# A planner's order table with one entry per task, token tiles laid one after another for layer A's transpose, and layer B's product as one operation per chunk

## The chip, the cores and the metric

The kernel runs on one core of one Trainium2 chip. Times are device microseconds (us) of one execution. The time before is a median of 360.13 us over 4 runs (359.67 to 361.37). One further reading of the same program is the profiled execution: the hardware profiler's trace of one run.

## The reference

The input x is 2048 tokens by 640 channels, in bf16. Four residual layers follow each other, A, B, A, B, each on a layer norm of x without learned factors. Both A layers have the same weights, and so have both B layers.

```python
x = x + A(layernorm(x)); x = x + B(layernorm(x))
x = x + A(layernorm(x)); x = x + B(layernorm(x))
# A: diagonal complex recurrence over the tokens
h_t = Lam_bar * h_{t-1} + B_bar @ u_t          # 640 complex states
A(u)_t = 2 * Re(C @ h_t) + Dskip * u_t
# B: gating by a signal that does not depend on x
kv = short_conv(B_k) * B_v                     # 4 taps per channel
y  = causal_conv(kv, ssm_k) + kv * ssm_D       # 2048 taps, by FFT in the reference
B(q) = q * y
```

So y is computed once and used by both B layers.

## The kernel before, in words

**Front part.** Tables of sines and cosines are made. k and v are loaded transposed, kv is formed by the short convolution (matmuls with diagonal matrices, L1064) and stored to memory. A's weights are transposed and combined on TensorE (L486, L501, L502, L522). The long convolution y is a two-stage transform over five groups of 128 channels, `yq0` to `yq4`: stage A (`KA`, `VA`, L1109, 64 columns a matmul), stage B (`KB`, `VB`, L1133 to L1138), the product of the spectra on VectorE (`pw`, L1190 to L1195), the inverse stages (`IB`, L1214 and L1215; a DMA transpose `tt`; `IA`, L1243), and a store (`st`). Every result of TensorE is copied out of one of four PSUM buffers by ScalarE (L296) or VectorE (L298).

**Layers.** x is cut into four chunks of 512 tokens, c0 to c3, each held as four tiles q = 0 to 3 of 128 tokens by 640 channels. `A1` and `A2` are the two A layers, `B1` and `B2` the two B layers. For one chunk, an A layer (`ALayer.chunk`) runs these tasks:

- `ln`: statistics. In A1 by batch-norm instructions on VectorE (`bn`, L620 and L621), elsewhere by squares summed on ScalarE (`nm`, `sq`, `sd`, L590 to L600); `post` on VectorE gives 1/std and -mean/std;
- `id`: the normalised tile, on ScalarE (L640) or VectorE (L642), written to a buffer `u`;
- `tu`: one DMA transpose of `u` to `uT` (L670), issued by SyncE;
- `bp`: three groups of matmuls with B_bar (L684, L687), 100 matmuls of 256 columns for a chunk; `ev` copies them out on ScalarE (L296);
- `ri`, `sc`, `cy`, `ro` on VectorE: a rotation (L706 to L708), two scans along the tokens (L722), the carry to the next chunk (L733 to L735), a rotation back (L745 to L747);
- `cp`: the output product for each tile (L773), 30 matmuls for an even tile and 25 for an odd one, two more in A1, where x is added on TensorE too;
- `xe`: the new x tile out of PSUM, with its sum (L781, L783, L785).

A B layer (`b_chunk`) runs `ln`, then `u` for each tile (the same normalisation, L640 or L642), then `m`: a product with y (L818, 128x640) and an addition of x (L820 with its sum in B1, L822 in B2). In the last chunk of B2 each tile is a group by itself, with two fused operations, L805 and L809. SyncE then stores the output (L828).

**What sets the order.** All of this is written down as tasks with dependencies, an engine (for copies, `id`, `u` and A1's `xe` a choice of two: ScalarE first, VectorE second) and an estimated duration. `Sched.run` (L179) is a list planner that runs while the kernel is built: it walks through planned time, and at each moment gives every free engine the ready task of the highest rank. A task with a choice goes to its second engine only if the first one is busy for 0.3 more planned us. The planner also gives out the shared buffers (13 of b5, 6 of b10, 4 PSUM). Then all tasks are emitted in the order of their planned starts. On the chip each engine executes its own list strictly in that order; an instruction whose inputs are late holds up everything behind it on that engine. The rank comes from the table `WHEN` (L52), which before has one number for each group: tasks whose names differ only behind a colon, such as the tiles of `A1c0_cp`, share one.

Of the kernel before, what the change touches and what calls it, by code (L numbers as in the profile page):

```python
# [9 lines left out]
ALU = mybir.AluOpType  # L10
# [23 lines left out]
TOK = 2 * NB  # L34
# [18 lines left out]
    "yt_io0": -1077.9, "yt_ph0": -1019.3, "yt_sin0": 190.5, "yt_neg0": 314.5, "yt_io6": -1435.7, "yt_ph6": -1019.8, "yt_sin6": -1080.4, "yt_neg6": 172.3,  # L53
    "yt_io12": 294.3, "yt_ph12": -1069.6, "yt_sin12": 375.6, "yt_neg12": 156.6, "yt_Ci": 118.7, "yt_Si": 403.1, "yt_nsi": 236.7, "yt_f0": -965, "yt_f2":
    -1540, "yt_f3": -1887, "yt_f4": 179, "yt_h0": 174.5, "yt_h1": 154.3, "yt_h2": 148.5, "yt_h3": 189.9, "kv_dsl": 34.9, "kv_kd": 410.2, "kv_k0": -1067.5,
    "kv_k1": 205.4, "kv_k2": 230.3, "kv_d0": -1030.9, "kv_d1": -1037.8, "kv_d2": 125.1, "kv_ds0": 95.3, "kv_lk0": -919.4, "kv_lv0": 119.4, "kv_mm0":
    -1408, "kv_ev0": 192.8, "kv_st0": -966.5, "kv_ds1": 400.8, "kv_lk1": 143.9, "kv_lv1": 406.3, "kv_mm1": 238.5, "kv_ev1": 232.1, "kv_st1": 180.1,
    "kv_ds2": -1696.5, "kv_lk2": 390.3, "kv_lv2": 173.4, "kv_mm2": 244.3, "kv_ev2": 403.7, "kv_st2": -1020, "kv_ds3": -1063.8, "kv_lk3": -1121.4,
    "kv_lv3": 669.8, "kv_mm3": 420.7, "kv_ev3": -1025, "kv_st3": 1400.2, "kv_ds4": 90.8, "kv_lk4": -926.2, "kv_lv4": 7.3, "kv_mm4": 33, "kv_ev4": -831.9,
    "kv_st4": -980.1, "a_pl": 481.2, "a_p0": -840.7, "a_p1": -1244.2, "a_p2": 1659, "a_p3": 156.5, "a_p4": -793.6, "a_p5": 225.8, "a_p6": -1643.5,  # L60
    "a_lamd": 156.7, "a_f": 165.3, "a_dd": 521.1, "a_ldB0": 150.8, "a_ldB1": -1247.6, "a_wl00": -1403.1, "a_wc00": -1264.8, "a_wm00": 209.8, "a_wl01":
    75.8, "a_wc01": -881, "a_wm01": 418.7, "a_wl02": 307.9, "a_wc02": 301.4, "a_wm02": 403.5, "a_wl03": 164, "a_wc03": -903.2, "a_wm03": -1083.3,
    "a_wl04": 357.2, "a_wc04": -1099.8, "a_wm04": 601.7, "a_b00": 178, "a_b0e0": 230.3, "a_b01": 173.9, "a_b0e1": -1067.1, "a_b10": 69.2, "a_b1e0":
    -1516.7, "a_b11": -1560.6, "a_b1e1": 508.8, "a_gm0": -1359.9, "a_ge0": -1048.3, "a_gm1": -727, "a_ge1": -1525.1, "a_gm2": -1618.5, "a_ge2": -1376.9,
    "a_gm3": -1641.8, "a_ge3": -1386.3, "a_gm4": -1643.2, "a_ge4": -1403, "a_wl10": -2.6, "a_wc10": 155, "a_wm10": -1068.5, "a_wl11": 159.1, "a_wc11":
    -965.4, "a_wm11": 184, "a_wl12": -818.1, "a_wc12": -1242.6, "a_wm12": 79.5, "a_wl13": 104.8, "a_wc13": 414.8, "a_wm13": 181.4, "a_wl14": -1008.6,
    "a_wc14": 26.2, "a_wm14": -1248.1, "a_ti": -1521.4, "a_ta": 395.3, "a_t0": -829.9, "a_t1": 170.8, "a_t2": 613.8, "yq0_kl": -982.4, "yq0_ka": -1602.5,
    "yq0_KA": 159.8, "yq0_KB": 402.8, "yq0_vl": -1113.3, "yq0_VA": 481.3, "yq0_VB": -1118.9, "yq1_kl": 30, "yq1_ka": 311.3, "yq1_KA": -1517.3, "yq1_KB":
    -954.5, "yq0_pw": 209.4, "yq0_IB": 298.2, "yq0_tt": -1552, "yq1_vl": 1519.1, "yq1_VA": -1096.8, "yq1_VB": 420.6, "yq0_IA": 407.6, "yq0_st": -1537.5,
    "yq2_kl": 435.6, "yq2_ka": 157.2, "yq2_KA": 277.9, "yq2_KB": -1166.2, "yq1_pw": 360.8, "yq1_IB": -871.2, "yq1_tt": -1130.5, "yq2_vl": -1467.1,  # L70
    "yq2_VA": 23.2, "yq2_VB": 25.8, "yq1_IA": -1377.8, "yq1_st": -1484.6, "yq3_kl": 498, "yq3_ka": 1686.9, "yq3_KA": 438.7, "yq3_KB": -1402.5, "yq2_pw":
    1355.7, "yq2_IB": -1302.1, "yq2_tt": -1424, "yq3_vl": -834.2, "yq3_VA": 161.1, "yq3_VB": 86.9, "yq2_IA": 2.9, "yq2_st": 300.2, "yq4_kl": -1275,
    "yq4_ka": 618.1, "yq4_KA": -931.8, "yq4_KB": 225.6, "yq3_pw": -1643.5, "yq3_IB": 331.5, "yq3_tt": -814.8, "yq4_vl": -798.8, "yq4_VA": 157.4, "yq4_VB":
    326.4, "yq3_IA": 628.2, "yq3_st": 404.5, "yq4_pw": 594.6, "yq4_IB": 599.4, "yq4_tt": -1071.8, "yq4_IA": 126.1, "yq4_st": -1404, "xl0": -1622.2,
    "A1c0_ln_bn": 302.5, "A1c0_ln_sd": -1096.7, "A1c0_ln_post": -1648.8, "A1c0_id": -1304.5, "A1c0_tu": -1475.7, "A1c0_bp": 10.7, "A1c0_ev": 355.4,
    "A1c0_ri": 62.1, "A1c0_sc": 641.6, "A1c0_cy": 233.1, "A1c0_ro": -1576.9, "A1c0_xr": 396.2, "A1c0_cp": 627.9, "A1c0_xe": -1443.8, "xl1": -978,
    "A1c1_ln_bn": 221, "A1c1_ln_sd": 479.8, "A1c1_ln_post": -942.2, "A1c1_id": 1422.5, "A1c1_tu": -1312.3, "A1c1_bp": 338.4, "A1c1_ev": 192.1, "A1c1_ri":
    1654.8, "A1c1_sc": -1000.3, "A1c1_cy": -1122.1, "A1c1_ro": -1077.3, "A1c1_xr": 627.3, "A1c1_cp": -1539.8, "A1c1_xe": -1077.9, "xl2": -1346.1,
    "A1c2_ln_bn": 611.3, "A1c2_ln_sd": -1123.4, "A1c2_ln_post": 402.2, "A1c2_id": 141, "A1c2_tu": 96.1, "A1c2_bp": 640.8, "A1c2_ev": -867.9, "A1c2_ri":
    22, "A1c2_sc": 40.1, "A1c2_cy": -1431.1, "A1c2_ro": -1012.6, "A1c2_xr": 471.5, "A1c2_cp": -1082.5, "A1c2_xe": -1450.9, "xl3": 672.8, "A1c3_ln_bn":  # L80
    37.8, "A1c3_ln_sd": -1392.7, "A1c3_ln_post": -1339.6, "A1c3_id": 30.4, "A1c3_tu": 252.1, "A1c3_bp": -1329.6, "A1c3_ev": 410.6, "A1c3_ri": -1152.5,
    "A1c3_sc": 383.7, "A1c3_ro": 185.7, "A1c3_xr": 534.8, "A1c3_cp": 257.2, "A1c3_xe": -1166.6, "yl0": 143.2, "B1c0_ln_nm": 627.2, "B1c0_ln_sq": 628.8,
    "B1c0_ln_sd": 604.7, "B1c0_ln_post": 185.1, "B1c0_u": -1662.7, "B1c0_m": 369.5, "A2c0_ln_nm": 202.2, "A2c0_ln_sq": 222, "A2c0_ln_sd": 59.4,
    "A2c0_ln_post": -1459.4, "A2c0_id": 273.5, "A2c0_tu": 215.4, "A2c0_bp": 72.8, "A2c0_ev": -1459.1, "A2c0_ri": -790.3, "A2c0_sc": -1361.1, "A2c0_cy":
    -1371.9, "A2c0_ro": -1371.9, "A2c0_cp": 348.7, "A2c0_xe": 634.5, "yl1": 669.8, "B1c1_ln_nm": 308.3, "B1c1_ln_sq": 369.1, "B1c1_ln_sd": 59.5,
    "B1c1_ln_post": 617.9, "B1c1_u": 409, "B1c1_m": -805.6, "A2c1_ln_nm": -1007.9, "A2c1_ln_sq": 422.1, "A2c1_ln_sd": 197.3, "A2c1_ln_post": 131.4,
    "A2c1_id": 423.7, "A2c1_tu": 550.3, "A2c1_bp": 151.8, "A2c1_ev": 590.1, "A2c1_ri": -1014.6, "A2c1_sc": -1015.2, "A2c1_cy": -1015.5, "A2c1_ro": 641.4,
    "A2c1_cp": 487.2, "A2c1_xe": -1744.8, "yl2": -1648.1, "B1c2_ln_nm": 322.3, "B1c2_ln_sq": -1642.8, "B1c2_ln_sd": -1510.7, "B1c2_ln_post": 363.6,
    "B1c2_u": -1565.4, "B1c2_m": 451.1, "A2c2_ln_nm": -1048.9, "A2c2_ln_sq": -1744.2, "A2c2_ln_sd": -1039.1, "A2c2_ln_post": -1411.3, "A2c2_id": 441.9,
    "A2c2_tu": -901.5, "A2c2_bp": 358.9, "A2c2_ev": 451.8, "A2c2_ri": -1675.7, "A2c2_sc": 417.5, "A2c2_cy": 416.1, "A2c2_ro": 419.3, "A2c2_cp": 1402.8,  # L90
    "A2c2_xe": -1034.4, "yl3": -1423.8, "B1c3_ln_nm": -1629.1, "B1c3_ln_sq": 195.9, "B1c3_ln_sd": 600.5, "B1c3_ln_post": 593.8, "B1c3_u": -1463.1,
    "B1c3_m": -1491.8, "A2c3_ln_nm": 219.3, "A2c3_ln_sq": 213.9, "A2c3_ln_sd": 213.1, "A2c3_ln_post": 1658, "A2c3_id": 370.7, "A2c3_tu": 233.6, "A2c3_bp":
    365.2, "A2c3_ev": 436.9, "A2c3_ri": 205.6, "A2c3_sc": -1741.5, "A2c3_ro": -918.5, "A2c3_cp": 442.7, "A2c3_xe": 185.4, "B2c0_ln_nm": 221.3,
    "B2c0_ln_sq": 220.8, "B2c0_ln_sd": -957.2, "B2c0_ln_post": 407.7, "B2c0_u": -1559.8, "B2c0_m": -1667.9, "B2c0_st": 424.7, "B2c1_ln_nm": -1255,
    "B2c1_ln_sq": -954.9, "B2c1_ln_sd": -1008.5, "B2c1_ln_post": -1038.2, "B2c1_u": 19.7, "B2c1_m": -1027.2, "B2c1_st": 212.6, "B2c2_ln_nm": 615.6,
    "B2c2_ln_sq": 624.8, "B2c2_ln_sd": 623.5, "B2c2_ln_post": -798.2, "B2c2_u": 238.2, "B2c2_m": 219.3, "B2c2_st": -982.6, "B2c30_ln_nm": 169.5,
    "B2c30_ln_sq": -1093.7, "B2c30_ln_sd": 99.3, "B2c30_ln_post": 219.3, "B2c30_u": 435.4, "B2c30_m": -841.8, "B2c31_ln_nm": 196.4, "B2c31_ln_sq":
# [547 lines left out]
class ALayer:  # L645
# [6 lines left out]
    def chunk(self, c, src, sums_in, x_ready, resid, s_x, sums_out, src_slot, reload):  # L652
# [786 lines left out]
```

## Time and profile before

| quantity | value |
|---|---|
| median of the 4 runs | 360.13 us |
| time of the profiled execution | 359.94 us |
| span of the profiled execution, first to last instruction | 358.2 us |
| TensorE busy | 326.5 us, 91% |
| VectorE busy | 321.8 us, 90% |
| ScalarE busy | 253.2 us, 71% |
| mean granted TensorE clock | 0.985 |

"Busy" is the time in which an engine executes, as a share of the span. "Granted clock" is the share of TensorE's full clock rate that its clock gate allowed. Groups of instructions in the profile are named by the line of the kernel that issued them; lines L296, L298, L640 and L642 lie in helpers that several tasks use. Matmuls overlap in the array, so the spacing between the starts of two matmuls, and not the duration of one, is what each adds. On VectorE, too, the start of the next instruction can lie ahead of the recorded end, so sums along an engine go by the spacing of starts.

### The profile page before, as it was taken

The page shows a single profiled execution, that of the slowest core. Times are in us where ns is not written, and L with a number is a line of the kernel's source. Part 1 is how long each engine was busy: PE and PEld are TensorE (multiplying, and loading weights), DVE is VectorE, ACT ScalarE, POOL GpSimd, SP SyncE. Part 2 cuts the span into 40 slices and gives each one's busy share as a digit, 9 for nine tenths or more (in the row PEclk, how much of TensorE's full clock was granted, in tenths as well). Part 3 has the DMA queues.
Part 4 walks back from the last instruction along what each step waited for, and adds up shares of the span by engine and source line. Part 5 has one row for each costly group of instructions (what it writes and reads, how often), then busy time and mean ns, then how long its engine had stood idle before and what let it go on. Part 6 is the DMA issues. An engine that isn't in the chain of part 4 may idle for free.

```text
span 358.2 us, 8317 instructions
## 1 busy us (share of the span) xinstructions
PE 326.5 (91%) x3493; PEld 243.0 (68%) x3493; DVE 321.8 (90%) x482; ACT 253.2 (71%) x399; POOL 24.5 (7%) x57
## 2 busy tenths in 40 slices
PE   2888899989997998999999999999999999999980
PEld 1357867866684888886776685688655788756550
DVE  8979999778799579989997998999999799999996
ACT  6589976989499999784598199796618681106861
POOL 6448210000000000000000000000000000000000
PEclk9999999999999899999999999999999999999995
DMA  8999999999997970966096622450032043000231
GB/s 201 222 195 177 197 181 222 221 164 220 228 234 142 219 163 2 144 123 205 2 206 147 267 76 51 116 127 2 15 60 76 0 112 112 1 2 0 82 140 73
DMA packets 118711, 45.90 MB, mean 128 GB/s; under 512 B 111629, under 2 KB 112914, under 8 KB 118674
## 3 DMA queue, kind: packets, MB, share of 16 engines
q1 hardware_dynamic: 118528, 45.36, 59.8%
q8 instruction: 27, 0.44, 0.5%
q14 instruction: 10, 0.08, 0.1%
q10 hardware_dynamic: 146, 0.01, 0.0%
HBM read 17.38 MB, written 7.86 MB: 70 GB/s over the span
## 4 chain that ended last, share of the span: by engine, by line
PE 59%; DVE 11%; ACT 11%; DMA 10%; POOL 3%; issue 3%; SPq 1%; ACTq 0%; POOLq 0%; DVEq 0%
PE ps L773 31%; PE ps L684 10%; PE ps L687 10%; DMA b<-b 6%; ACT b L296 6%; DMA b<-in_A_C_im_dram 4%; PE ps L1064 3%; ACT b L466 2%; DVE bs L620 2%; ACT b L640 1%; SPq L462 1%; PE ps L1243 1%; POOL b L401 1%; DVE b L809 1%; DVE b L805 1%
## 5 line engine op out<-in xcount | busy, mean ns | idle before, releaser
L296 ACT ACTIVATE b<-ps 128x1024 bf16<-128x1024 f32 (+3 forms) x121 | 106.0, 956 | 28.5 <-PE ps L687 22.7
L773 PEld LDWEIGHTS <-b 128*128 128x128 bf16 x880 | 67.6, 98 | 48.2
L773 PE MATMUL ps<-W,b 128*128 128x128 bf16 (+1 forms) x640 | 95.8, 299 | 0.0
L684 PE MATMUL ps<-b,BT 128*128 128x256 bf16 x400 | 57.8, 276 | 1.8 <-ACT b L296 1.0
L687 PE MATMUL ps<-b,BT 128*128 128x256 bf16 x400 | 57.5, 275 | 0.0
L722 DVE TENSOR_TENSOR_SCAN b<-rtab,b 128x1290 bf16<-128x1290 f32 x16 | 44.7, 2832 | 0.2
L684 PEld LDWEIGHTS <-BT 128*128 128x128 bf16 x400 | 39.1, 99 | 6.9 <-issue 1.1
L687 PEld LDWEIGHTS <-BT 128*128 128x128 bf16 x400 | 39.5, 99 | 4.9
L595 ACT ACTIVATE junk<-b,nmean 128x640 bf16<-128x640 f32 x48 | 39.8, 828 | 1.5
L640 ACT ACTIVATE b<-b,nmr,rstd 128x640 bf16<-128x640 f32 (+1 forms) x42 | 35.7, 916 | 3.0 <-DVE nmr L607 2.0
L1133 PE MATMUL ps<-b,b 128*128 128x128 bf16 x170 | 35.1, 219 | 1.6 <-ACT b L296 0.7
L1136 PE MATMUL ps<-b,b 128*128 128x128 bf16 x170 | 35.2, 219 | 0.0
L1138 PE MATMUL ps<-b,b 128*128 128x128 bf16 x150 | 32.8, 219 | 0.0
L1135 PE MATMUL ps<-b,b 128*128 128x128 bf16 x150 | 32.8, 219 | 0.0
L298 DVE CAST b<-ps 128x1024 bf16<-128x1024 f32 (+2 forms) x28 | 28.0, 1024 | 4.3 <-PE ps L1138 2.3
L781 ACT ACTIVATE b<-ps 128x640 f32<-128x640 f32 x15 | 10.5, 701 | 26.4 <-PE ps L773 26.4
L773 PE MATMUL ps<-G,b 128*128 128x512 bf16 (+1 forms) x160 | 27.0, 299 | 0.0
L1064 PE MATMUL ps<-b,fd 128*128 128x512 bf16 x80 | 20.3, 405 | 2.1 <-ACT b L296 1.1
L470 DVE SCALAR_TENSOR_TENSOR W<-b,s_F 128x640 bf16<-128x640 bf16 x20 | 17.2, 879 | 3.8 <-ACT b L466 3.6
L466 ACT ACTIVATE b<-b,s_F 128x640 f32<-128x640 bf16 x20 | 16.5, 832 | 5.7 <-DMA b<-in_A_C_im_dram 4.7
L590 ACT ACTIVATE nmean<-sums 128x4 f32<-128x4 f32 (+1 forms) x15 | 3.0, 201 | 22.7 <-DVE b L785 19.3
L1214 PE MATMUL ps<-b,b 128*128 128x128 bf16 x160 | 18.4, 219 | 0.5 <-ACT b L296 0.5
(210 smaller groups left out, 571.7 us busy)
## 6 DMA issues: line engine op xcount, KB each, us to landing
b<-in_A_x_dram SPq DMA_DIRECT2D x8, 640.0 KB, 6.0
b<-ysd SPq DMA_DIRECT2D x8, 640.0 KB, 4.1
b<-in_B_ssm_k_dram SPq DMA_DIRECT2D x5, 512.0 KB, 6.4
kvd<-b SPq DMA_DIRECT2D x5, 512.0 KB, 4.9
b<-kvd SPq DMA_DIRECT2D x5, 512.0 KB, 4.9
ysd<-b SPq DMA_DIRECT2D x5, 512.0 KB, 4.6
out_dram<-b SPq DMA_DIRECT2D x8, 320.0 KB, 2.2
W<-in_A_B_im_dram SPq DMA_DIRECT2D x1, 800.0 KB
```

The costliest lines, as they stand in the source:

```text
L296: nc.scalar.activation(out, in_, ACT.Copy)
L595: nc.scalar.activation(small.junk, src(q), ACT.Square, bias=st["nmean"][:, i:i + 1], scale=1.0, accum_out=st["ssq"][:, i:i + 1])
L640: nc.scalar.activation(dst, src, ACT.Identity, bias=st["nmr"][:, i:i + 1], scale=st["rstd"][:, i:i + 1])
L684: nc.tensor.matmul(pb[:, jj, c2, :], lhsT=aw["BT1"][:, c2, j, k, :], rhs=uT[:, k, 0:2, :].rearrange("p t i -> p (t i)"), start=(k == 0), s ...
L687: nc.tensor.matmul(pb[:, jj, c2, :], lhsT=aw["BT0"][:, c2, k, j * P:(j + 1) * P], rhs=uT[:, k, 2:4, :].rearrange("p t i -> p (t i)"), star ...
L722: nc.vector.tensor_tensor_scan(gv, rt, gv, 0.0, ALU.mult, ALU.add)
L773: nc.tensor.matmul(pc[:, o0:o1], lhsT=lh, rhs=rh, start=(n == 0), stop=(n == len(ops) - 1))
L1064: nc.tensor.matmul(pk[:, 512 * b:512 * (b + 1)], lhsT=s_ds.get()[:, l, :], rhs=kT[:, t0:t0 + 512], start=(l == 0), stop=(l == 3))
L1133: nc.tensor.matmul(ps[:, g, 0, :], lhsT=T["Cf"].get()[:, q, :], rhs=are, start=True, stop=single)
L1135: nc.tensor.matmul(ps[:, g, 0, :], lhsT=T["Sf"].get()[:, q, :], rhs=A[:, 2 * q + 1, :], start=False, stop=True)
L1136: nc.tensor.matmul(ps[:, g, 1, :], lhsT=T["NSf"].get()[:, q, :], rhs=are, start=True, stop=single)
L1138: nc.tensor.matmul(ps[:, g, 1, :], lhsT=T["Cf"].get()[:, q, :], rhs=A[:, 2 * q + 1, :], start=False, stop=True)
```

## The change

1. `WHEN` gets one entry for each task (with the part behind the colon), and the rank is that number alone; a pair also sets, for that task, how long the first engine must be busy before the second may take it (-1 lets it go at once, 99 in effect never). Task names in B's product and stores change with it.
2. The planner's estimates for some VectorE tasks are set to other values.
3. In A, `u` is laid out tile after tile (tile, channel block, channel) and no longer channel block by channel block with the four tiles inside. Each `id` then writes 640 adjacent elements instead of five runs of 128. The transpose keeps its shape of 20 blocks. The moving operand of `bp` becomes two runs of 128 columns, 640 apart, where it was one run of 256.
4. In B (but for the last chunk of B2), the four products of a chunk (4 x 128x640, L818) become one, `mm` (128x2560), which waits for all four `u`. The additions `m` stay one for each tile.

```diff
 WHEN = {
-    "A1c0_ln_bn": 302.5, "A1c0_ln_sd": -1096.7, "A1c0_ln_post": -1648.8, "A1c0_id": -1304.5, "A1c0_tu": -1475.7, "A1c0_bp": 10.7, "A1c0_ev": 355.4,
...
+    "A1c0_ln_bn": 94.5, "A1c0_ln_sd": 99.39, "A1c0_ln_post": 102.7, "A1c0_id:0": 104.6, "A1c0_id:1": (104.42, 6), "A1c0_id:2": 108.04, "A1c0_id:3":
...
-            t.rank = t.path + t.bias if WHEN is None else 0.001 * t.path - WHEN.get(t.name.partition(":")[0], 0)
+
+            t.rank, t.wait = t.path + t.bias, 0.3
+            if WHEN is not None:
+                when = WHEN[t.name]
+                t.rank, t.wait = (-when[0], when[1]) if isinstance(when, tuple) else (-when, 0.3)
...
-                cands = [t for t in ready if eng in t.engs and (t.engs[0] == eng or eng_free[t.engs[0]] > now + 0.3) and can(t)]
+                cands = [t for t in ready if eng in t.engs and (t.engs[0] == eng or eng_free[t.engs[0]] > now + t.wait) and can(t)]
...
-                ln_apply(nc, eng, st, q, s_u.get()[:, :, slot, :], src(q).rearrange("p (k e) -> p k e", e=P))
-            outs.append(S.add(f"{nm}_id:{q}", ("act", "dve"), (0.81, 0.85), [t_post], e_id, uses=[s_u, src_slot]))
+                ln_apply(nc, eng, st, q, s_u.get()[:, slot * D:(slot + 1) * D], src(q))
+            outs.append(S.add(f"{nm}_id:{q}", ("act", "dve"), (0.81, 0.52), [t_post], e_id, uses=[s_u, src_slot]))
...
-            nc.sync.dma_start_transpose(out=s_uT.get().rearrange("p k q i -> p (k q) i"), in_=s_u.get().rearrange("p k q e -> p (k q e)"))
+            nc.sync.dma_start_transpose(out=s_uT.get().rearrange("p q k i -> p (q k) i"), in_=s_u.get())
...
-                                             rhs=uT[:, k, 0:2, :].rearrange("p t i -> p (t i)"), start=(k == 0), stop=False)
+                                             rhs=uT[:, 0:2, k, :], start=(k == 0), stop=False)
...
-                def e_m(_, q=q, bu=bu):
-                    b, x = bu(), s_x.get()[:, q, :]
-                    nc.vector.tensor_tensor(b, b, s_Y.get()[:, q, :], ALU.mult)
...
+                def e_mm(_):
+                    b = s_b.get()
+                    nc.vector.tensor_tensor(b, b, s_Y.get(), ALU.mult)
+                t_mm = S.add(f"{nm}_mm", "dve", c_tt(4 * D), us + [y_ready], e_mm, uses=[s_b, s_Y])
```

The table decides the order, so the order is part of the change. These are the tasks on two engines where the prediction speaks of them, as the two programs have them once built.

TensorE around the first `bp`, before: `a_gm1, yq3_VA:m0, yq4_KA (4 groups), yq3_VA:m1 to m3, A1c0_bp:0, A1c0_bp:1`. After: `yq3_VA:m1, a_gm2, yq3_KB:m4, yq4_KA (4 groups), yq2_IA:m1, yq3_VB (5 groups), yq2_IA:m0, A1c0_bp:1, yq4_KB:m3, A1c0_bp:0`.

TensorE from `A1c3_cp` on, before: `A1c3_cp, A2c0_cp, A2c2_bp, A2c1_cp:0, A2c3_bp, A2c1_cp:2,1,3, A2c2_cp, A2c3_cp:0,2,1,3`; `A2c1_bp` stands ahead of `A1c3_cp`. After: `A1c3_cp, A2c1_bp, A2c0_cp:2, A2c2_bp:1,2, A2c0_cp:3, A2c2_bp:0, A2c0_cp:0,1, A2c1_cp:3,2, A2c3_bp, A2c2_cp:2, A2c1_cp:1,0, A2c2_cp:3,0,1, A2c3_cp:1,3,0,2`.

VectorE from the end of `A1c3_ro` on, after the change: `A2c1_ln_post, A2c1_id:2,1, B1c2_ln_post, B1c2_u:0,2, mm, m x4, A2c0_ri, sc, A2c2_ln_post, A2c0_ro` | `A2c0_cy, B1c3_ln_post, B1c3_u x3, mm, m x4, A2c1_ri, sc, ro` | `A2c0_xe:2,3, A2c1_cy, A2c3_ln_post, A2c2_ri, sc, cy, A2c0_xe:1,0, A2c2_ro` | `A2c1_xe:2, B2c0_ln_post, A2c1_xe:3, B2c0_u:0,2, mm, m x4, A2c3_ri, sc, A2c1_xe:1,0, A2c3_ro` | `A2c2_xe:2, B2c1_ln_post, A2c2_xe:3, B2c1_u:2, A2c2_xe:0,1, B2c1_mm, m:2,0, A2c3_xe:1, B2c1_m:1,3, B2c2_ln_post, A2c3_xe:3, B2c2_u:2, B2c31_ln_post, B2c2_u:1, B2c2_mm, m:1,2, A2c3_xe:0, B2c2_m:3, B2c33_ln_post, B2c2_m:0, A2c3_xe:2`, and behind it the last chunk of B2: `post, u, u, m, post, m, u, u, m, m`.

VectorE around chunk 2's statistics, before: `A1c1_id:1,2,3, A1c2_ln_bn, a_t2, A1c2_ln_post`, with `yq3_pw` behind them. After: `yq2_IA:e0, yq3_VB:e4, a_wm11:1, yq3_pw, A1c2_ln_bn, a_wm12:0, a_t2, A1c2_ln_post`. On SyncE the load of chunk 2, `xl2`, stands before the change behind `yq2_tt`, and after it behind `A1c1_tu` and `yq2_st`, whose data `yq2_IA:e0` writes.

## The prediction

> **What bounds the kernel now.** I read the page's table of busy time first, then its forty slices, then the stretches before and after TensorE becomes continuous.
>
> ```profile
> PE 326.5 (91%) x3493; PEld 243.0 (68%) x3493; DVE 321.8 (90%) x482; ACT 253.2 (71%) x399; POOL 24.5 (7%) x57
> PE   2888899989997998999999999999999999999980
> DVE  8979999778799579989997998999999799999996
> ```
>
> TensorE (PE) and VectorE (DVE) are both nine tenths full. The slices show where they aren't: at the start, in places up to slice 16, and in the last two. The busy time by stretch (start:end, length, then busy us and instructions on PE, PEld, DVE, ACT, POOL, then clock, DMA share, GB/s) gives amounts:
>
> ```profile
> 0.00:13.00 13.00, 4.28 (x31) 3.25 (x32) 11.33 (x35) 9.55 (x12) 9.05 (x24) 1.00 0.89 194
> 13.00:115.00 102.00, 92.49 (x1303) 70.44 (x1303) 89.19 (x135) 85.77 (x116) 15.40 (x34) 1.00 1.07 201
> 115.00:155.00 40.00, 37.78 (x468) 33.86 (x469) 31.89 (x48) 36.34 (x45) 0.00 (x0) 0.96 0.69 127
> 155.00:342.00 187.00, 186.37 (x1649) 132.17 (x1646) 176.67 (x242) 116.59 (x217) 0.00 (x0) 1.00 0.35 88
> 342.00:358.20 16.20, 5.55 (x48) 3.32 (x46) 12.75 (x26) 4.91 (x13) 0.00 (x0) 0.78 0.21 82
> ```
>
> From 155 to 342, TensorE is idle for 0.6 us in 187: this stretch can't be shortened, since the change takes no matmul away (both programs have 6979 TensorE instructions). Idle before 155 are 8.7, 9.5 and 2.2 us, and 10.7 after 342. From 13 to 115 the DMA engines are full (share 1.07), and their work is the same afterwards; the load of chunk 0, which starts layer A1, stands at nearly the same place of SyncE's queue in both. So I don't expect the first 99 us, up to A1's first statistics, to change much. What can be won lies between 99 and 155, and in the tail.
>
> Two places of that stretch, on TensorE's timeline (start, duration; in brackets the idle time before):
>
> ```profile
> 110.53 1.26 PE L1109 MATMUL ps<-FA,b 64*128 64x128 bf16 x32
> 112.31 0.40 PE L1109 MATMUL ps<-FA,b 64*128 64x128 bf16 x8 [0.52 <-ACT b L296]
> 113.12 0.62 PE L1109 MATMUL ps<-FA,b 64*128 64x128 bf16 x16 [0.41 <-DVE b L298]
> 114.25 0.40 PE L1109 MATMUL ps<-FA,b 64*128 64x128 bf16 x8 [0.51 <-DVE b L298]
> 115.39 1.23 PE L684 MATMUL ps<-b,BT 128*128 128x256 bf16 x5 [0.74 <-DMA b<-b]
> 116.41 1.27 PE L687 MATMUL ps<-b,BT 128*128 128x256 bf16 x5
> ```
>
> and on VectorE's:
>
> ```profile
> 118.14 1.62 DVE L642 TENSOR_SCALAR b<-b,rstd,nmr 128x640 bf16<-128x640 bf16 x3
> 123.83 0.89 DVE L620 BATCH_NORM_STATS2 bs<-b 128x6 f32<-128x320 bf16 x2 [4.06 <-DMA b<-in_A_x_dram]
> ```
>
> In 110.53 to 115.39, 4.86 us, TensorE does 64 stage-A matmuls. They follow each other by 27.5 ns (x16 less x8: 0.62 - 0.40 over 8), so 1.8 us of work: 3.1 us are lost, first to PSUM copies, then to A1c0's transposed tokens. And the clock has dropped: five matmuls of 256 columns take 1.02 us start to start (115.39 to 116.41) where they take 0.55 in the steady part; the starts up to 119.25 give another 1.7 us of loss. Together 4.8. VectorE meanwhile waits 4.06 us for x of chunk 2.
>
> So by these rows the clock halves after a sparse stretch with no gap over 0.74, and filling the stretch saves both parts. [...]
>
> **The change, part by part.**
>
> *Product in one operation.* A product of 128x640 (L818) takes 0.53 us to the next start (275.63 to 276.16 on VectorE's timeline), four 2.1; a bf16 product of 128x2560 (L707) 1.45. Seven chunks: -4.5 us of VectorE. It waits for four `u`, where a first product waited for one; behind it in VectorE's queue stand the four additions (0.75 each), and ScalarE's next statistics wait for these. The last two `u` on ScalarE take 1.8 us, so a wait is at most about that, and it costs nothing while TensorE has products of other chunks queued (it has, 155 to 342).
>
> *Tiles one after another.* An `id` on VectorE from f32, in runs of 128, takes 0.87 (3.48 for four); a `u` of the same size in one run 0.64. From bf16 in runs it takes 0.55; in one run the trace has only a larger operation, 0.45 for 1290 elements (L566), so at most 0.45 and, if time went by elements alone, 0.22; I take 0.4, near the row. VectorE has 11 `id` before (six bf16, five f32, 7.7 us) and 11 after (eight and three, some 5.1): -2.6. On ScalarE both layouts take 0.91. [...] For `bp`, two runs of 128 columns replace one of 256. Matmuls of 128 columns start 55.5 ns apart (L1214, 104.09 to 104.15), twice that is 111 against 109.2 for 256 columns: at worst 1.8 ns on each of 800, 1.4 us on TensorE; at best nothing. I take nothing and keep 1.4 for the range. The DMA transpose moves the same 20 blocks: 0.
>
> *Engine choices.* In the built order, `u` on VectorE go from 11 to 16 (+3.2 us), A1's `xe` there from 1 to 0 (-0.9), and PSUM copies change by +3 (`IA`, 1.2 each), -1, -2, +2, -1, with about +3. Estimates only steer the planner: 0. VectorE's sum: -4.5 - 2.6 + 3.2 - 0.9 + 3 = -1.8, half a per cent. ScalarE gives up some 5 us (five `u` of 0.91), which nobody waits for after 155 (it is 62% busy there). No engine is relieved enough to matter: the time hangs on the **order**.
>
> *Order, 99 to 155.* Before, four `yq4_KA` stand on TensorE directly ahead of `A1c0_bp`, whose tokens take 5.06 us from the issue of the transpose (110.28, in the chain of waits). After, `yq2_IA:m1`, five groups of `yq3_VB` and `yq2_IA:m0` lie between: 64 matmuls at 56 ns (spacing of L1214, same shape) and 32 in 1.1 us (L1243 at 67.56, in the chain), 4.7 us. So the wait of 0.74 is covered and the PSUM copies have time. But these groups need copies too, so I don't count all of 4.8: **-3.2**, two thirds, with 0 and -4.8 as ends. The load of chunk 2's x moves behind `yq2_IA:e0`; between it and A1c2's statistics VectorE now has `yq3_pw`, six operations of 1.28 us, 7.7 in all, against 5.4 from issue to data (118.47 to 123.83). The wait of 4.06 is covered; it was VectorE's and reached TensorE only through the gaps of 2.0 us between 140 and 160 (18.01 busy in 20). I take **-0.7** of these 2.0.
>
> *Order, before 99.* `yq2_pw` waits 1.83 us for a transpose (91.40). The new order may shift this either way: from -5 (half the 9.5 us idle in 13 to 115) to +2. I take **-0.8**, near the one wait that the row names.
>
> *Tail.* Before, the last `xe` starts at 348.20 and the span ends at 358.2: 10.0 us. After it, in the new order: `xe` 0.75, two `post` 0.36 each, eight fused operations of 0.80 (L805, L809), 7.9 us, and from VectorE's end to the span's end 3.2 as now (354.99 to 358.2): 11.1, so **+1.1**. ScalarE's squares for the last tile (0.20 + 0.83 + 0.19 + 0.29, 1.5 us) lie beside three of the fused operations.
>
> **Does VectorE keep up?** With `cp` of the layers interleaved, each output product waits for the `ro` of its chunk. Sums of spacings along both lists (`ri` 4.33, `sc` 6.07, `ro` 4.36, `cy` 0.37, `xe` and `m` 0.75, `u` 0.64, `post` 0.41; `cp` 4.06 even and 2.98 odd in A2, 15.2 for four in A1, `bp` 10.9), from A1c3_ro to A2c0_ro, A2c1_ro, A2c2_ro and A2c3_ro: VectorE 22.6 + 21.9 + 18.9 + 23.9 = 87.3; TensorE between the products that wait for them 26.1 + 25.1 + 18.0 + 21.1 = 90.3. So TensorE stays the longer by 3.0 us. Before, VectorE needs 92.6 us for this way (237.0 to 329.6), 3.2 of it waiting. With the same waits it needs 90.5: a tie, and it enters with a lead, since `A1c3_cp` starts on TensorE at 253.9 before, 17 us after `A1c3_ro`, less the 10.9 of `A2c1_bp`, which moves behind it: about 6. I count no stall.
>
> **Sum.** -3.2 - 0.7 - 0.8 + 1.1 = -3.6 on the profiled execution's 359.94 (span 358.2, the rest around it stays): **356.3 us**. The median of the runs, 360.13, is 0.2 above that execution; I leave this out.
>
> **The rivals.**
>
> *All gaps close* (0.10). TensorE loses nothing from 99 to 155: -4.8 - 2.0, and -3 more ahead of 99, +1.1: 351.2. For it: ScalarE and VectorE have spare time there. Against it: ScalarE is 36.3 of 40 busy in 115 to 155, and copies need it.
>
> *The gain is given back* (0.13). The front gives its 4.7, but VectorE's lead doesn't suffice, and its 3.2 us of waits reach TensorE, at A2c2_cp:2 above all (its link is short by 0.9, 18.0 against 18.9); with the tail's 1.1: 359.5, no change. For it: the tie above. Against: the lead of 6.
>
> *Slower, through one late copy in front* (0.21). After, more of y's work stands ahead of layer A1: A1c0's rotation (134.5 on VectorE before) moves behind `yq3_pw`, 7.7 us. If what goes ahead ran no denser than before, A1's chain of four scans, each bound to the one before by `cy`, starts 7.7 us later, and `A1c0_cp`, at 164 on TensorE before, finds TensorE with its y work done: an idle stretch of up to 7.7, less the 4.7 us of `yq4_IB` and `yq4_IA` still left to lie beside it, plus 1.7 for the clock: some +4.5. It decides once the rotation starts later than about 140. With +1.1 and nothing won: 365.5; with the 3.2 won, 362.3. Against it: the work that goes ahead has to be done anyway, and fills gaps there.
>
> That the order is not what the table wants is no case: the built lists are what I counted from.
>
> **How the numbers follow.** About 0.3% (1.1 us) is what a measurement of this kernel can tell from no change. Forecast, 352 to 359.0: 0.56. All gaps close: 0.10. Given back, 359.0 to 361.2: 0.13. Slower: 0.21, of which some 0.08 above 363. So faster 0.66, same 0.13, slower 0.21. The range runs from 350.0 (351.2 and a little of the unknown 1 to 2 us ahead of 99) to 363.0 (inside the slower case, or the forecast with the 1.4 of `bp` and the loss of 2 ahead of 99 and a stall); some 0.05 lie below and 0.10 above.
>
> **What would show it.** Right: no half clock between 105 and 155; VectorE's wait for x of chunk 2 under 1 us; TensorE continuous from 155 or sooner; the last `xe` about 5 us earlier than 348.2 and 11 before the end. Wrong: A1c0's rotation later than 140, a TensorE wait of over 1 us on L747 before an L773, `bp` spaced wider than 0.55 for five, or a first batch-norm well off 99.

## The result, and the profile after

The changed kernel took 361.29 us (median; 358.39 to 363.04), the kernel before 360.44 beside it: ratio 1.0019, 95% interval 1.0009 to 1.0029. That is slower by 0.2%, inside the 0.3% that the prediction takes as no change, and not the forecast's 1% less. The profiled execution took 362.22 us, with a span of 360.5 and a mean granted clock of 0.975.

The page of the changed kernel, in the same rows as before (busy time of the engines; forty slices of 9 us; the granted clock in tenths):

```profile
PE 327.9 (91%) x3493; PEld 244.6 (68%) x3493; DVE 322.2 (89%) x465; ACT 248.4 (69%) x395; POOL 24.4 (7%) x57
PE   0886998989998998999999999999999999999970
DVE  8998787997599988999996998979959989899896
PEclk9997899999999999899999999999999999999995
```

Slices are counted from 0. TensorE's slice 12 has gone from 7 tenths to 8, but a hole has opened in slice 3, and the clock dips twice, in slices 3 and 4 and in slice 16. The busy time by stretch (columns as in the prediction):

```profile
13.00:115.00 102.00, 92.27 (x1279) 71.55 (x1278) 87.73 (x122) 86.70 (x117) 17.04 (x36) 0.97 1.00 199
115.00:155.00 40.00, 37.33 (x499) 33.29 (x497) 37.23 (x52) 38.23 (x49) 0.00 (x0) 0.96 0.80 140
155.00:342.00 187.00, 187.00 (x1656) 133.84 (x1653) 171.03 (x224) 110.49 (x210) 0.00 (x0) 1.00 0.31 80
```

From 155 on TensorE never stops (187.00 of 187.00): VectorE keeps up. So the time was lost earlier. The starts of the same tasks in both traces say where:

| start of | before | after | difference |
|---|---|---|---|
| `yq0_pw` on VectorE | 44.19 | 47.77 | +3.58 |
| `yq1_pw` | 68.50 | 72.28 | +3.78 |
| first batch-norm of A1 | 98.99 | 102.80 | +3.81 |
| A1c0's rotation | 134.52 | 144.39 | +9.87 |
| last operation of A1c0's rotation back | 160.11 | 158.37 | -1.74 |
| last `xe` | 348.20 | 349.56 | +1.36 |
| end of the span | 358.20 | 360.48 | +2.28 |

The first 44 us lose 3.6 us, and all the way to the first batch-norm nothing of this comes back. The order behind it wins 2.45 (3.81 - 1.36), and the tail costs 0.92. These are two single executions: the profiles differ by 2.28 us, the medians by 0.85. The changed kernel's profile is of one of its slower executions (13 of them, at clocks of 0.975 and 0.976, took 362.2 to 363.0).

Inside the first 44 us, VectorE's timeline of the changed kernel, then GpSimd's and TensorE's ("..." marks rows left out):

```profile
27.23 3.23 DVE L633 TENSOR_SCALAR b<-rtab 128x1290 f32<-128x1290 f32 x1 [0.26 <-ACT rtab L627]
30.49 1.53 DVE L634 SCALAR_TENSOR_TENSOR b<-b,rtab 128x1290 f32<-128x1290 f32 x1
31.94 0.81 DVE L379 CAST BT<-ps 128x640 bf16<-128x640 f32 x1
```

```profile
26.33 3.40 POOL L482 TENSOR_TENSOR b<-ident_bf,s_lam 128x1920 bf16<-128x1920 bf16 x1 [0.74 <-DVE s_lam L476]
```

```profile
29.66 0.44 PE L567 MATMUL ps<-ident_bf,tab 128*128 128x128 bf16 x5 [0.41 <-ACT b L377]
...
32.81 0.29 PE L582 MATMUL ps<-b,W 128*128 128x128 bf16 x1 [1.85 <-DVE BT L379]
...
33.99 1.03 PE L1203 MATMUL ps<-FA,b 64*128 64x128 bf16 x16
```

L633 and L634 are one task, `a_t0`: it rounds the angles of A's rotation tables, and only `a_t1`, some 90 us later, needs it. It holds VectorE for 4.7 us (27.23 to 31.94). Behind it stand two copies out of PSUM, `a_b0e0:3` and `a_b0e0:2`. The kernel has four PSUM buffers, so TensorE waits 1.85 us for the first copy. Its clock is at half from 31.8 to 38.6: 16 stage-A matmuls take 1.03 us, where they took 0.62 before. The same places in the kernel before, on VectorE, GpSimd and TensorE:

```profile
29.93 1.99 DVE L552 TENSOR_SCALAR b<-rtab 128x1290 f32<-128x1290 f32 x1
31.95 1.53 DVE L553 SCALAR_TENSOR_TENSOR b<-b,rtab 128x1290 f32<-128x1290 f32 x1
```

```profile
27.83 3.40 POOL L401 TENSOR_TENSOR b<-ident_bf,s_lam 128x1920 bf16<-128x1920 bf16 x1 [1.73 <-DVE s_lam L395]
```

```profile
31.28 0.22 PE L501 MATMUL ps<-b,W 128*128 128x128 bf16 x1 [1.24 <-POOL b L401]
...
37.03 0.62 PE L1109 MATMUL ps<-FA,b 64*128 64x128 bf16 x16
```

In that order two more copies stood ahead of `a_t0`, and TensorE's wait (1.24 us, at 31.28) ended on GpSimd.

### The profile page after: what moved, and what is told of

Its sections match the earlier page's. It is cut to its first block, busy times and chain, and to the rows that moved or that the text cites. A ratio compares the mean times of both kernels' runs of the same rounds, so it can differ in the third digit from the quotient of the medians.

```text
span 360.5 us, 8273 instructions
## 1 busy us (share of the span) xinstructions
PE 327.9 (91%) x3493; PEld 244.6 (68%) x3493; DVE 322.2 (89%) x465; ACT 248.4 (69%) x395; POOL 24.4 (7%) x57
## 2 busy tenths in 40 slices
DMA packets 118711, 45.90 MB, mean 127 GB/s; under 512 B 111629, under 2 KB 112914, under 8 KB 118674
## 4 chain that ended last, share of the span: by engine, by line
PE 66%; DVE 15%; ACT 8%; DMA 6%; issue 3%; DVEq 0%; POOL 0%; POOLq 0%; ACTq 0%
PE ps L854 33%; PE ps L765 11%; PE ps L768 11%; DMA b<-b 4%; ACT b L377 4%; PE ps L1158 2%; DMA b<-in_B_k_dram 2%; PE ps L1308 2%; DVE bs L701 2%; PE ps L1309 1%; PE ps L1203 1%; ACT b L547 1%; DVE b L1287 1%; DVE b L1286 1%; DVE b L1284 1%
## 5 line engine op out<-in xcount | busy, mean ns | idle before, releaser
L379 DVE CAST b<-ps 128x1024 bf16<-128x1024 f32 (+1 forms) x29 | 31.0, 1082 | 6.8 <-PE ps L1203 5.0
L1227 PE MATMUL ps<-b,b 128*128 128x128 bf16 x170 | 35.1, 219 | 1.2 <-ACT b L377 0.7
L1230 PE MATMUL ps<-b,b 128*128 128x128 bf16 x170 | 35.3, 219 | 0.0
L721 ACT ACTIVATE b<-b,nmr,rstd 128x640 bf16<-128x640 f32 (+1 forms) x37 | 31.8, 910 | 2.4 <-DVE nmr L688 2.4
L1232 PE MATMUL ps<-b,b 128*128 128x128 bf16 x150 | 32.8, 219 | 0.0
L1229 PE MATMUL ps<-b,b 128*128 128x128 bf16 x150 | 32.8, 219 | 0.0
L1203 PE MATMUL ps<-FA,b 64*128 64x128 bf16 x320 | 14.5, 229 | 5.9 <-ACT b L377 3.0
L1308 PE MATMUL ps<-b,b 128*128 128x128 bf16 x160 | 19.1, 219 | 0.8 <-ACT b L377 0.5
L1309 PE MATMUL ps<-b,b 128*128 128x128 bf16 x160 | 19.1, 219 | 0.0
```

Source lines behind the costliest of these rows:

```text
L379: nc.vector.tensor_copy(out, in_)
L721: nc.scalar.activation(dst, src, ACT.Identity, bias=st["nmr"][:, i:i + 1], scale=st["rstd"][:, i:i + 1])
L1227: nc.tensor.matmul(ps[:, g, 0, :], lhsT=T["Cf"].get()[:, q, :], rhs=are, start=True, stop=single)
L1229: nc.tensor.matmul(ps[:, g, 0, :], lhsT=T["Sf"].get()[:, q, :], rhs=A[:, 2 * q + 1, :], start=False, stop=True)
L1230: nc.tensor.matmul(ps[:, g, 1, :], lhsT=T["NSf"].get()[:, q, :], rhs=are, start=True, stop=single)
L1232: nc.tensor.matmul(ps[:, g, 1, :], lhsT=T["Cf"].get()[:, q, :], rhs=A[:, 2 * q + 1, :], start=False, stop=True)
```

## The experiments

My theory: the place of `a_t0` costs the 3.8 us, and the order behind the first batch-norm does win. Rivals: the new operations cost the time; the half clock alone does; some other bound of the front does. Each kernel ran beside the kernel before; the ratio is to that. "TensorE's end" is the end of its last matmul, and the half clock of the last 10 us (from 351.0 before, from 352.6 in the changed kernel) is left out. All columns but the last are of one profiled execution each.

| kernel | `yq0_pw` | `yq1_pw` | first batch-norm | from it to TensorE's end | span | half clock | ratio, 95% |
|---|---|---|---|---|---|---|---|
| before | 44.19 | 68.50 | 98.99 | 248.6 | 358.2 | 115.4-118.9 | 1 |
| after | 47.77 | 72.28 | 102.80 | 246.7 | 360.5 | 31.8-38.6, 144.4-147.8 | 1.0019 (1.0009-1.0029) |
| late_t0 | 43.53 | 72.83 | 103.28 | 245.4 | 359.7 | 54.3-61.1 | 1.0029 (1.0010-1.0047) |
| fill_b0 | 45.51 | 71.45 | 102.10 | 247.1 | 360.1 | 55.3-58.7, 144.0-147.4 | 1.0027 (1.0009-1.0045) |
| order_only | 46.86 | 72.80 | 102.98 | 245.5 | 359.4 | 33.0-36.4, 56.9-60.3 | 1.0041 (1.0021-1.0062) |
| t0_yq2 | 43.52 | 68.05 | 97.72 | 245.4 | 354.1 | none | 0.9926 (0.9901-0.9951) |
| t0_ev2 | 43.60 | 72.04 | 102.88 | 245.5 | 359.3 | 53.5-60.3 | 1.0001 (0.9985-1.0017) |
| t0_before | 44.52 | 69.71 | 101.41 | 247.9 | 359.9 | none | 1.0012 (0.9995-1.0030) |
| t0_oldops | 43.65 | 68.18 | 98.40 | 245.4 | 354.8 | none | 0.9937 (0.9913-0.9960) |
| t0_fill | 43.52 | 68.05 | 98.73 | 245.5 | 355.2 | none | 0.9912 (0.9886-0.9938) |
| front_bn2 | 43.88 | 67.97 | 98.83 | 251.4 | 361.2 | 114.8-121.6, 145.5-148.9 | 1.0066 (1.0039-1.0092) |

**late_t0: `a_t0` behind `yq0_pw`.**

```diff
         order.sort(key=lambda t: (t.start, t.idx))
+        late = next(t for t in order if t.name == "a_t0")
+        order.remove(late)
+        order.insert(next(i for i, t in enumerate(order) if t.name == "yq0_pw") + 1, late)
```

> The changed kernel with one task moved: `a_t0` (two VectorE operations of 3.23 and 1.53 us at 27.23, ahead of the PSUM copies `a_b0e0:3` and `a_b0e0:2`) is emitted behind `yq0_pw` instead. Theory (the order of the first 44 us costs what the later order wins): the two copies start near 27.2 instead of 31.94, TensorE's wait of 1.85 us at 32.81 goes, no half clock between 32 and 39, `yq0_pw` at 43.5 to 45.5 instead of 47.77, the first batch-norm of A1 1 to 4 us before 102.80, and the time 358.0 to 360.0. Rival (the new layout or the joined product costs the time): nothing before 99 us matters for the sum, 361.3 within 0.5. Rival (the half clock comes from something else than this stall): the clock still drops before 40 and `yq0_pw` stays later than 46.5.

`yq0_pw` came at 43.53, as the theory has it, but `yq1_pw` did not move: 360.76 us. VectorE and TensorE of this kernel (lines are 3 higher than in the changed one):

```profile
51.84 0.83 DVE L636 TENSOR_SCALAR b<-rtab 128x1290 f32<-128x1290 f32 x1
52.70 1.50 DVE L637 SCALAR_TENSOR_TENSOR b<-b,rtab 128x1290 f32<-128x1290 f32 x1
54.12 1.22 DVE L1167 TENSOR_TENSOR b<-ps,b 128x1024 bf16<-128x1024 f32 x1
```

```profile
55.39 1.46 PE L1206 MATMUL ps<-FA,b 64*128 64x128 bf16 x24 [3.90 <-DVE b L1167]
```

The same loss has moved on by 23 us: now `kv_ev2:1` (L1167) stands behind `yq0_pw` and `a_t0`, TensorE waits 3.90 us for its PSUM buffer, and the clock halves from 54.3. The theory in its first form, that the place ahead of `a_b0e0:3` is bad, is too narrow: what counts is which copy stands behind.

**fill_b0: TensorE kept busy in the hole, `a_t0` where it was.**

```diff
                 for j in range(NJ):
-                    nc.tensor.matmul(pb[:, j, :], lhsT=B[c][:, j, k * P:(k + 1) * P], rhs=ident[:], start=True, stop=True)
+                    for _ in range(4 if c == 0 and k in (2, 3) else 1):
+                        nc.tensor.matmul(pb[:, j, :], lhsT=B[c][:, j, k * P:(k + 1) * P], rhs=ident[:], start=True, stop=True)
```

> The changed kernel with the ten matmuls of `a_b00:2` and `a_b00:3` each issued four times with the same operands and result: 30 matmuls more, 1.7 us at 55.5 ns, on TensorE between 28.8 and 31.5, where it waits anyway. No copy and no order is changed. Theory that the clock follows how full TensorE is: no half clock at 32 to 39, the ten matmuls of `a_b11:1` at 55 ns instead of 106 ns, `yq0_pw` 1.5 to 3 us before 47.77, time 358.8 to 360.3. Rival (the late copies alone delay the front, the clock does not matter): `yq0_pw` within 0.7 of 47.77, time 361.3 within 0.5. If the clock drops all the same, fullness of TensorE is not its condition, and the time is 361.3 to 362.0.

No half clock at 32 to 39, and `yq0_pw` 2.26 us earlier: in this execution 30 matmuls more ahead of 31.8 were enough for the full clock. Two lines of its TensorE:

```profile
32.80 0.23 PE L583 MATMUL ps<-b,W 128*128 128x128 bf16 x1 [1.38 <-DVE BT L379]
...
33.46 0.62 PE L1204 MATMUL ps<-FA,b 64*128 64x128 bf16 x16
```

The wait is still there (1.38), the 16 stage-A matmuls are back at 0.62. Against `t0_yq2` (43.52) the 4.25 us of the changed kernel at `yq0_pw` so split into 2.26 of clock and 1.99 of late copies. But the time, 360.66, moved little: TensorE then waits 1.62 us for `kv_ev2:1`, the clock halves at 55.3, and only 0.8 us of the gain reach `yq1_pw`.

**order_only: both operation changes undone, order kept.**

```diff
-                ln_apply(nc, eng, st, q, s_u.get()[:, slot * D:(slot + 1) * D], src(q))
+                ln_apply(nc, eng, st, q, s_u.get()[:, :, slot, :], src(q).rearrange("p (k e) -> p k e", e=P))
...
-                    b = s_b.get()
-                    nc.vector.tensor_tensor(b, b, s_Y.get(), ALU.mult)
+                    for q in range(4):
+                        b = s_b.get()[:, q, :]
+                        nc.vector.tensor_tensor(b, b, s_Y.get()[:, q, :], ALU.mult)
...
```

> The changed kernel's order and engine choices with both operation changes undone: tokens in runs of 128 across four tiles as before, and four products in a row in place of the joined one. Theory (front order; VectorE has room): the first 100 us as in the changed kernel (`yq0_pw` 47.8, first batch-norm 102.8); VectorE has 7 us more to do after 105, of which it has 16 free between 155 and 342: 361.3 to 363.5. Rival (the new operations cost the time, by `bp` on rows in pieces or the join that waits for four `u`): faster than 361.0, down to 359.

361.18: the time of the changed kernel, and the same late front (72.80, 102.98). VectorE is busy 325.0 us against 322.2, so 2.8 us more and not the 7 expected, and from 155 to 342 it has room for that:

```profile
155.00:342.00 187.00, 186.01 (x1622) 133.16 (x1639) 174.39 (x245) 110.38 (x210) 0.00 (x0) 1.00 0.31 82
```

So the operations neither cost nor save anything that these runs can tell: the two intervals, 1.0021 to 1.0062 and 1.0009 to 1.0029, overlap.

**front_yq0, after_again, front_bn: an order written out.** To put the order of one kernel's front ahead of the other's rest, I replaced the planner's walk by a list of tasks and engines; `front_yq0` and `front_bn` take the list of the kernel before up to `yq0_pw` and up to A1c0's batch-norm, `after_again` the changed kernel's own.

```diff
-        while len(order) < len(tasks):
...
+        while todo:
+            blocked.clear()
+            for i, (t, e) in enumerate(todo):
+                if e not in blocked and can(t):
+                    break
+                blocked.add(e)
...
+            todo.pop(i)
+            take(t, e)
```

> The changed kernel, its tasks emitted in the order and on the engines of the kernel before up to `yq0_pw`, and in its own order after that. Theory (front order): `yq0_pw` at 43.7 to 45.0, no half clock before 44, first batch-norm of A1 at 98.5 to 100.5, and all of the 2.6 us between it and TensorE's end kept: 357.0 to 359.3. Rival (new operations cost the time): 361.3 within 0.5, since the operations are the changed ones. Rival (the front's gain is eaten by a later wait, for instance the transposes of y): `yq0_pw` early, but the first batch-norm later than 101.5, time over 360.

> The changed kernel once more, with the same instructions in the same order on every engine, as a control on the chip of the two runs beside it: 361.3 within 0.6; `yq0_pw` near 47.8 and the first batch-norm of A1 near 102.8, as in its first profile.

> The changed kernel's operations, with the order and engines of the kernel before up to A1c0's first batch-norm and the changed kernel's order after it; the cut lies where both orders have emitted nearly the same tasks (at `yq0_pw`, where the first such kernel was cut, they had not). Theory (the front loses 3.8 us, the order after 99 wins 2.6, the two are independent): first batch-norm at 98.5 to 100, from it to TensorE's end 246 to 247.5, time 357.3 to 359.3. Rival (the new order after 99 lives on work that its own front had done): from the batch-norm to TensorE's end 248.5 or more, time 359.8 to 362.

371.21, 366.57 and 369.50 us (1.0314, 1.0175, 1.0253). The control condemns the group: the order on every engine is that of the changed kernel, and it takes 5 us more. The one difference is which buffer a task gets: the list gave out the buffer whose last user was emitted first, the planner the one that it expects to be free first. From 100 to 152, VectorE of `after_again` waits 5.1 us in copies whose buffer a DMA transpose still uses, waits that the changed kernel does not have:

```profile
DVE b L422 <- DMA b<-b: 5.1, 2, 3.4
```

No conclusion on the order is drawn from these three.

**front_bn2: the same cut, buffers as the planner would give them.**

> Again the changed kernel's operations with the order and engines of the kernel before up to A1c0's first batch-norm and the changed kernel's order after it, but now with the buffers handed out as the two kernels' own planners do; the first such kernels handed them out in another rotation, and the control with that rotation and an unchanged order took 5 us more. Theory (the front loses 3.8 us, the order after 99 wins 2.6, the two are independent): first batch-norm at 98.5 to 100, from it to TensorE's end 246 to 247.5, time 357.3 to 359.3. Rival (the new order after 99 lives on work that its own front had done): from the batch-norm to TensorE's end 248.5 or more, time 359.8 to 362.

362.36, and the rival is right: the first batch-norm comes at 98.83, as in the kernel before, but from it to TensorE's end it takes 251.4 us, more than either kernel. ScalarE of this kernel and of the changed one, in the first 5 us from the batch-norm and in the 5 us from 20 us after it (the fourth pair of numbers):

```profile
98.83:103.83 5.00, 4.95 (x75) 4.39 (x75) 4.83 (x16) 3.59 (x6) 0.00 (x0) 1.00 0.47 140
118.83:123.83 5.00, 5.00 (x75) 4.98 (x73) 2.60 (x4) 3.14 (x4) 0.00 (x0) 0.72 0.98 113
```

```profile
102.80:107.80 5.00, 5.00 (x80) 4.46 (x77) 4.83 (x16) 4.98 (x7) 0.00 (x0) 1.00 0.97 186
122.80:127.80 5.00, 4.68 (x50) 4.13 (x47) 4.66 (x5) 4.97 (x6) 0.00 (x0) 1.00 1.11 199
```

In the changed kernel ScalarE is busy for 48.4 of the 50 us behind the batch-norm; here for 46.5, and it idles 3.3 us in these two stretches. Between them it is full, TensorE waits 2.0 us for its copies (at 113.33 and 115.32), and the clock is at half from 114.8 to 121.6. So "front" and "rest" cannot be exchanged as I had thought. That the new order after 99 needs copies which its own front had made fits these rows; which copies they are is not shown.

**t0_yq2: `a_t0` ahead of `yq2_pw`.**

```diff
+        order.insert(next(i for i, t in enumerate(order) if t.name == "yq2_pw"), late)
```

> The changed kernel with `a_t0` (4.8 us of VectorE) moved from 27.2 to directly ahead of `yq2_pw`, where VectorE waits 3.8 us for a transpose; behind `yq0_pw` it had delayed the copy of `kv_mm2:1`, for whose PSUM buffer TensorE then waited 3.9 us. Theory (order of the front, and that copy): `yq0_pw` at 43.0 to 44.5, no TensorE wait above 2 us between 44 and 72, `yq1_pw` at 68 to 70, first batch-norm of A1 at 98.7 to 101, time 357.5 to 359.5. Rival (something else between 44 and 72, a load or the copies as a whole, holds `yq1_pw` whenever `yq0_pw` comes): `yq1_pw` at 71.5 to 73, time 360.3 to 361.5.

357.78 us, 0.9926 (0.9901 to 0.9951): faster than both kernels, by moving one task. `yq0_pw` at 43.52, `yq1_pw` at 68.05, the batch-norm at 97.72, and the longest TensorE wait from 44 to 72 is 1.62 us. Its page and VectorE's timeline:

```profile
PE   0888979989998898999999999999999999999970
...
PEclk9999999999999999999999999999999999999995
```

```profile
86.54 0.82 DVE L636 TENSOR_SCALAR b<-rtab 128x1290 f32<-128x1290 f32 x1
87.40 1.50 DVE L637 SCALAR_TENSOR_TENSOR b<-b,rtab 128x1290 f32<-128x1290 f32 x1
90.12 1.29 DVE L1287 TENSOR_TENSOR b<-b,b 128x2176 bf16<-128x2176 bf16 x1 [1.22 <-DMA b<-b]
```

The hole in slice 3 is gone, and `a_t0` lies in VectorE's wait for the transpose, of which 1.22 are left of the changed kernel's 3.82:

```profile
95.20 1.29 DVE L1284 TENSOR_TENSOR b<-b,b 128x2176 bf16<-128x2176 bf16 x1 [3.82 <-DMA b<-b]
```

The profiled execution of `t0_yq2` was the fastest of its runs, 355.83, at a clock of 0.988; the others have 0.983 to 0.985 and took 357.6 to 357.9.

**t0_ev2: `a_t0` one task later than in late_t0.**

```diff
+        order.insert(next(i for i, t in enumerate(order) if t.name == "kv_ev2:1") + 1, late)
```

> The changed kernel with `a_t0` behind `kv_ev2:1`, that is one instruction later on VectorE than in the run that put it behind `yq0_pw` (360.8), and far ahead of the run that put it before `yq2_pw` (357.8). Theory (what `a_t0` costs is the copy that TensorE waits for behind it, wherever that is): the wait for `kv_ev2:1` falls from 3.9 back to about 1.6 us, but the copies of `yq1_VA` and `yq0_IB` on VectorE come 4.8 us later: `yq0_pw` 43.5, `yq1_pw` 69.5 to 72, time 358.3 to 360.3. Rival (only the copy of `kv_mm2:1` mattered): `yq1_pw` 68 to 69, 357.0 to 358.2.

359.91, between the two, as the theory has it (its interval overlaps that of `late_t0`). TensorE's longest wait from 44 to 100 falls from 3.90 to 1.62, which `t0_yq2` has too, another of 1.47 comes behind it, and the clock still halves from 53.5:

```profile
56.10 0.29 PE L1312 MATMUL ps<-b,b 128*128 128x128 bf16 x1 [1.47 <-DVE b L989]
```

L989 is no copy; it makes a table that these matmuls read. So it is not the one copy: what stood behind `a_t0` and was needed next differed in all three bad places.

**t0_before: the same move in the order before.**

> The kernel before, with the same one task moved: `a_t0` from 29.93 on VectorE to directly ahead of `yq2_pw`. Theory (`a_t0` hurts only where it stands ahead of copies that TensorE waits for, as in the changed order; in the order before, TensorE's wait at 31.28 ends on GpSimd, not on a copy): 359.2 to 360.6, `yq0_pw` at most 1.5 us earlier than 44.19. Rival (any order gains when `a_t0` goes into VectorE's wait ahead of `yq2_pw`, so the changed order has no merit of its own): 357.0 to 358.7, `yq0_pw` at 41 to 42.5.

360.90, ratio 1.0012 (0.9995 to 1.0030): nothing is won there. TensorE's wait at 31.6 still ends on GpSimd:

```profile
31.61 0.22 PE L504 MATMUL ps<-b,W 128*128 128x128 bf16 x1 [1.24 <-POOL b L404]
```

So the changed order has a merit of its own, and `a_t0` hid it. The place is also a poorer one here: VectorE's wait ahead of `yq2_pw` was 1.83 us in the kernel before, `a_t0` takes 2.3 there, and `yq2_pw` and the first batch-norm come 2.4 later than before.

**t0_oldops: t0_yq2 with both operation changes undone.** The edits are those of `order_only`.

> The changed kernel with `a_t0` ahead of `yq2_pw`, and both operation changes undone (tokens in runs of 128 across four tiles, four products in a row). Theory (VectorE has room after 155, the operations are worth nothing in time): 357.8 within 0.7. Rival (with the front mended VectorE becomes the bound, and its 7 us come back in part): 359 to 361.

358.18 (0.9937, against 0.9926 for `t0_yq2`; the intervals overlap). VectorE does 2.0 us more from 150 to 336 (173.36 against 171.33), and TensorE is busy for 185.0 of 186 in both. Even with the front mended the operations give nothing that can be measured.

**t0_fill: t0_yq2 with `yq4_VA`'s matmuls issued twice.**

```diff
-                for o4 in range(4):
+                for o4 in list(range(4)) * (2 if name == "yq4_VA" else 1):
```

> The changed kernel with `a_t0` ahead of `yq2_pw`, and the 64 stage-A matmuls of `yq4_VA` issued twice with the same operands and result: 1.8 us more on TensorE, in the stretch before A1c1's `bp` where it is busy for 1.6 of 3 us and waits for ScalarE's copies. Without the repeat five of six runs had a mean granted clock of 0.983 to 0.985 and took 357.6 to 357.9, one had 0.988 and took 355.8. Theory (clock follows how full TensorE is): the clock is 0.987 or more in most runs, median 355.5 to 357.0. Rival (the repeated matmuls are paid in full, or the clock drops elsewhere): 357.8 to 359.6.

357.03 (0.9912; 356.47 to 358.19), clocks from 0.983 to 0.991, five of six at 0.987 or more. The clock fits the theory, the time lies just outside its 355.5 to 357.0, and its interval overlaps that of `t0_yq2`, so it is not settled whether the repeat pays.

## Why the prediction was wrong, point by point

- **Order, before 99** (-0.8, ends -5 and +2): the step that failed. It is +3.81, outside even the ends, and the sign that I had named, a first batch-norm well off 99, came (102.80). I had one row for 99 us, the wait ahead of `yq2_pw`, which grew from 1.83 to 3.82 us, and did not go along VectorE's new list between. There the list shows `a_t0` directly ahead of two PSUM copies, and the trace of before had its price: 1.99 + 1.53 us, in place of the 2.2 that the kernel's planner counts for it. One task moved takes the 3.81 to -1.27 (`t0_yq2`). Part of the 3.81 is the half clock of this one execution: at `yq0_pw` 2.26 of 4.25 (`fill_b0`).
- **The premise for it, that DMA fills 13 to 115 and so the front will not change**, was wrong: the share was 1.07 before and 1.00 after, with the same 45.90 MB in all, and 0.14 from 60 to 65 in the changed kernel. A high share of a queue's time did not mean that the queue was what the others waited for.
- **Order, 99 to 155** (-3.2 and -0.7): right in kind, short in size here. From the batch-norm to the last `xe` -2.45 where I had -3.9. The wait ahead of `A1c0_bp` fell from 0.74 to 0.32, but a half clock came back at 144.4, in a sparse stretch that the kernel before has too (0.94 of wait at 143.31), there without a half clock: 16 stage-A matmuls with 0.90 of wait ahead of them, and then `bp` at 1.02 us for five, the spacing that I had named as a sign of failure:

```profile
143.35 0.62 PE L1203 MATMUL ps<-FA,b 64*128 64x128 bf16 x16 [0.90 <-ACT b L377]
144.27 0.94 PE L1203 MATMUL ps<-FA,b 64*128 64x128 bf16 x16 [0.29 <-ACT b L377]
145.18 1.23 PE L765 MATMUL ps<-b,BT 128*128 128x256 bf16 x5
146.20 1.27 PE L768 MATMUL ps<-b,BT 128*128 128x256 bf16 x5
```

  The six profiles of this order without that half clock need 245.4 or 245.5 from the batch-norm to TensorE's end, the two with it 246.7 and 247.1: 1.2 to 1.7 us. Against the 248.6 of before, which has one of its own, the order is then worth 3.1; against the order before without one (`t0_before`, 247.9), 2.4.
- **VectorE's wait for x of chunk 2** (under 1 us): 1.2, from 4.06.
- **Tail** (+1.1): +0.92, right.
- **VectorE keeps up**: right, no TensorE wait from 155 to 342. So the rival "the gain is given back" (359.5, up to 361.2) is close in time and has the wrong mechanism: the gain is given away ahead of it, not at A2's products.
- **The slower rival** (decides once A1c0's rotation is later than 140): the rotation came at 144.4, and nothing followed; TensorE is continuous from 145, for the y work that went ahead had indeed to be done anyway. The condition was no test, and that its 362.3 lies near the measured time is luck.
- **Product in one operation** (-4.5) and **tiles one after another** (-2.6): nearly as sized, without effect on the time. By the starts, the products of the seven chunks take 14.6 us before and 10.7 after, -3.9; 2.7 of this comes from standing in a row (11.8 in `order_only`), 1.2 from the join. The 23 `id` and `u` save 2.3 by the new layout (14.2 to 11.9). `bp` at full clock is not spaced wider than 0.55.

## What to carry to other kernels

When an order is replaced, walk the new list of each engine from the start, and ask of every long operation which copy out of PSUM stands behind it and which matmul waits for that buffer; a task that nobody needs for 90 us belongs into a wait of its engine that is long enough for it, not ahead of such a copy. A high busy share of the DMA engines (1.07 here, from 13 to 115) is no proof that they are the bound; look for who waits for a DMA. And two orders can't be judged by stretches: what the one gains behind a point may rest on what it did ahead of it.

## What the runs showed of the hardware

**A VectorE operation that took longer beside a GpSimd operation.** The same 1290-element f32 operation took 0.82 us at 86.5 in `t0_yq2` and 0.83 at 51.8 in `late_t0`, with GpSimd idle (0.00 us busy from 84 to 88, and from 50 to 55), but 1.99 in the kernel before and 3.23 in the changed one. There a GpSimd operation of 3.40 us ran beside it, and VectorE's ended 0.7 us after that one's end both times (31.23 to 31.92, 29.73 to 30.46). So 1.2 and 2.4 us of `a_t0` lie inside the instruction, where no wait view shows them; what held it there is not shown.

**Half clocks came behind stretches in which TensorE was busy for about half the time.** By the modelled ends, TensorE was busy for 1.72 of the 3.41 us (0.50) ahead of the half clock at 31.8, for 1.97 (0.58) ahead of 144.4, and in the kernel before for 1.48 (0.43) ahead of 115.4. Not every such stretch has one behind it: 55.70 to 59.10 in the changed kernel (1.78 of 3.40) has none, and neither has 137 to 140 in `t0_yq2` (1.60 of 3.00) and in `t0_fill` (1.85 of 3.00). What decides between them, these rows don't show. The half clocks at 115.4 and 144.4 lasted 3.41 us, the one at 31.8 lasted 6.83. The runs of the changed kernel show how the time goes with the clock: three with a mean clock of 0.988 or 0.989 took 358.4 to 358.8 us, less than the kernel before, and the thirteen at 0.975 or 0.976 took 362.2 to 363.0. Which of the half clocks the three were without, no profile shows.

**Which buffer is used can cost more than the order.** With an unchanged order, another rotation of the buffers took 5 us more (`after_again`, 366.57 against 361.29); 5.1 us of VectorE's waits are in copies into buffers that a transpose still used.
